# Three changes to the expert stage of an attention, FFN and expert kernel on one Trainium2 core: who makes a weight chunk's low part, who multiplies the first shares, and when weight sums are issued

## The chip, the cores and the metric

The program runs on one core of a Trainium2 chip. TensorE (PE) multiplies matrices, VectorE (DVE), ScalarE (ACT) and GpSimd (POOL) work element by element, and SyncE (SP) and POOL issue DMA transfers. The metric is the device time of one execution in microseconds. Several runs of a kernel are made and the median is taken.

## The reference

Three layers follow each other, each feeding the next. A clustered attention gives `x` of 1536 x 512. A feed-forward layer follows (512 to 2048 to 512). The third is a mixture of eight experts, and the change is in it:

```python
def _moe2_ref(x, w_gate, w1, w2) -> np.ndarray:
    N, D = x.shape
    E = w_gate.shape[1]
    logits = x @ w_gate
    logits = logits - logits.max()
    P = np.exp(logits)
    for _ in range(8):
        P /= P.sum(1, keepdims=True) + 1e-09
        P /= P.sum(0, keepdims=True) + 1e-09
        P *= N / E
    out = np.zeros((N, D), dtype=np.float32)
    for e in range(E):
        h = np.maximum(x @ w1[e], 0.0)
        ye = h @ w2[e]
        out += P[:, e:e + 1] * ye
    return out.astype(np.float32)
```

Here N = 1536, D = 512, E = 8, and w1 is 8 x 512 x 1024, w2 is 8 x 1024 x 512. The eight rounds of normalising P are called the sinkhorn steps below; a "share" is an element of P, the weight of a token for an expert.

## The kernel before

The expert stage takes the span from about 567 us to its end. It computes in fp32 out of fp32r products: each operand is split in a high part (a cast, on ACT) and a low part (the difference, an element-wise subtraction), and a product is three matmuls, high x high, high x low and low x high. Names begin with `wh`/`wl` for the first weight, `vh`/`vl` for the second, `gh`/`gl` for the activations.

The stage has 16 blocks k: two halves of the tokens (sb = k // 8), eight experts each (e = k % 8). A block has four units u. In each unit the two-by-two block product x @ w1 is made out of seven products of sums of blocks (a Strassen-like scheme); they are the seven `l1_group` calls (line 1038, six matmuls of 128x384 each), and their results leave the banks by ACT copies `c00`, `c22`, `c03`, `c44` (line 1047) and DVE sums `XA` (line 1059); `c00` and `c03` share one buffer. ACT applies the relu (lines 1057, 1061). The first weight comes in three chunks per unit, A, B, C, with two, two and three blocks of 128x256. `w1_load` (SP) fetches them, in part from sums of weights (T1 to T4) kept in DRAM, and `w1_split` makes the high part on ACT (line 967) and the low part (line 968): on DVE for A and B, on POOL for C. In even units chunk C is one tile `wf` and one operation of 128x768, in odd units two tiles (`w1r`), operations of 128x256 and 128x512.

The second layer uses seven products again. `w2_load` (SP) and `w2_add` (an accumulating DMA issued by POOL, line 992) bring the weight blocks, `w2_split` makes `vh` on ACT (line 997) and `vl` on POOL (line 998, 128x512), `g_sum` forms sums `XS`/`XA` of the activations on DVE (lines 72 and 74, 128x768), `g_split` makes `gh` on ACT (line 1018) and `gl` on DVE (line 1019, 128x768). `l2_piece` (line 1075) multiplies and DVE adds the result, times the share, to the output tile `x` (lines 1091, 1093, 1097).

For block 0 the shares are not ready when its results are, so these are stored unscaled (line 1091) and multiplied later by the shares `Pt` or their negatives `Nt`: `first_share` (line 1105), 12 products of 128x256, after the last sinkhorn step (lines 878 to 892 on DVE, and line 887 on PE, for the column sums `cs`/`cp`).

The sums of weights of the experts 4 to 7 are made by `t_step` during the first blocks: SP loads a block into a tile (`ts` for the first weight, `w2r` for the second), POOL issues a DMA that adds another block (line 227), SP stores the sum to DRAM (`td`, line 223), and so on through the list `STEPS`; a "+" stands for an accumulating DMA, a "T" for a store:

```python
STEPS = (
    ("B11", "+B12", "T1", "+B22", "T2", "+B21", "T4", "B12", "+B22", "T3"),
    ("B11", "+B12", "+B22", "T2", "+B21", "T4"),
)
```

The order of the work is set by a table: `do(t, fn, ...)` enters each piece with a place t, the table is sorted, and the pieces are emitted in that order; 28 places make a block, 7 a unit, one an `l1_group`. From the emitted order a scheduler makes the order of each engine. `behind_pe` keeps a DMA behind the last PE instruction emitted before it. Each engine then works through its list in order and waits where something is missing.

Of the kernel before, what the change touches and what calls it, by code (L numbers as in the profile page):

```python
# [7 lines left out]
F32 = mybir.dt.float32  # L8
# [3 lines left out]
AF = mybir.ActivationFunctionType  # L12
ALU = mybir.AluOpType
# [7 lines left out]
def attention_moe_moe2(ctx, tc, v, qt, kt, centroids, w_in, w_out, w_gate, w1, w2, eye, out, dbg=None):  # L21
    nc = tc.nc
# [16 lines left out]
    wp = ctx.enter_context(tc.tile_pool(name="wp", bufs=1))  # L39
# [208 lines left out]
    def w1_tiles(ch, par, nm, pool="mp"):  # L248
        sh = [P, 3 if ch == "C" else 2, KC // 2 * P]
        WT[ch] = [  # L250
            slot_pool[pool].tile(sh, F32R, tag=f"w{t}{ch}{par}", name=f"w{t}{ch}{nm}", bufs=1) for t in "hl"
        ]
        return WT[ch]

    def w1_use(T):
        return {name: T[ch] + [n] for ch in T for n, name in enumerate(MEMBERS[ch])}
# [450 lines left out]
    for i in range(NHALF):  # L707
        g = i // 4
        for t in range(HT):
            n = 6 * i + 2 * t - LEAD  # L710
# [6 lines left out]
        for s in range(NT):  # L717
            n = 6 * i + s
# [117 lines left out]
    Pt = mp.tile([P, B * NT, E], F32, tag="Pt", name="Pt", bufs=1)  # L836
    Nt = mp.tile([P, B * NT, E], F32, tag="Nt", name="Nt", bufs=1)
# [123 lines left out]
    def w1_split(k, u, ch):  # L961
        h, l = T = w1_tiles(ch, 0, f"m{k}_{u}")
        n = 0
        for src in WR[u % 2, ch]:
            m = src.shape[1]
            hs = h[:, n : n + m, :]
            nc.scalar.copy(hs, src)
            (nc.gpsimd if ch == "C" else nc.vector).tensor_tensor(l[:, n : n + m, :], src, hs.bitcast(F32), ALU.subtract)
            n += m
        W1U.setdefault((k, u), {}).update(w1_use({ch: T}))  # L970

# [129 lines left out]
    def first_share(r, c):  # L1101
        yv = xt[0].rearrange("p k s -> p (k s)").rearrange("p (m d) -> p m d", d=DM)
        for m in range(r * HT, (r + 1) * HT):
            acc = yv[:, m, c * 256 : (c + 1) * 256]
            nc.vector.tensor_scalar(acc, acc, (Nt if c else Pt)[:, m, 0:1], None, ALU.mult)

    XBLK = x_blocks(xt[1])
    XD = tc.dram_tile([len(COMBOS), P, 2, FH], F32, name="xd")
# [41 lines left out]
    def do(t, fn, *args):  # L1150
        ev2.append((t, len(ev2), fn, args))
# [4 lines left out]
    for k in range(NB):  # L1156
        for u in range(4):
            t0 = t1[k] + 7 * u
            if k or u:
                for ch, d in (("A", -12), ("B", -11), ("C", -10)):  # L1160
                    do(t0 + d, w1_load, k, u, ch)
                for ch, d in (("A", -4.6), ("B", -2.6), ("C", 0.05)):
                    do(t0 + d, w1_split, k, u, ch)
            for i in range(7):
                do(t0 + i, l1_group, k, u, i)
                if k == E - 1 and u == 3:
                    do(t0 + i + 0.9, xc_ready, PROD[i][0])
        if k == E - 1:
            for name, d in (("S1", 14), ("S2", 17), ("S4", 20.4)):
                do(t1[k] + d, xc_load, name)  # L1170
        S0 = t1[k] + G1
        sp = G1 / 14
        for p in range(2):
            r = t1[k] + 16 if p == 0 else S0 + 0.3
            for n, name in enumerate(("S1", "S2", "S3")):
                do(r + (1.0 if p == 0 else 0.25) * n, g_sum, k, name, p)
            do(S0 + 7 + 2 * p, g_sum, k, "S4", p)
        first = split_at.setdefault(k, [])
        for j in range(14):
            t = S0 + sp * (j - 3) + 0.2 if j >= 4 else S0 + 2 * j - 5.8  # L1180
            first.append(max(t, t1[k] + 9))
        for i in range(7):
            b, i_ = divmod(7 * k + i - 3, 7)
            t = split_at[b][2 * i_ + 1] + 0.15 if b >= 0 else -1
            do(t, w2_load, k, i)
            if PROD[i][1] in ("T1", "T3"):
                do(min(t + 4.4, first[2 * i] - 3.6), behind_pe, w2_add, k, i)
        for j in range(14):
            i, p = divmod(j, 2)
            do(first[j], w2_split, k, i, p)  # L1190
            do(first[j] + 0.1, g_split, k, i, p)
            for n in range(3):
                do(S0 + sp * j + sp * n / 3 + 0.01, l2_piece, k, i, p, n)
    for c, jobs in enumerate(JM):
        for j, job in enumerate(jobs):
            for n in range(len(STEPS[job[0]])):
                do(2 + 14 * c + 46 * j + 4.4 * n, behind_pe, t_step, ("gp", "wp")[c], *job, n)
    for t, fn, name in (
        (143, xc_sum, "S1"), (145, xc_sum, "S3"), (147, xc_sum, "S2"), (151, xc_sum, "S4"),
        (191, xc_halves, "A11"), (196, xc_halves, "A12"), (201, xc_halves, "A22"), (206, xc_halves, "S3"),  # L1200
# [2 lines left out]
    for n, q in enumerate(((0, 0), (0, 1), (1, 1), (1, 0))):  # L1203
        do(56.6 + 2.4 * n, first_share, *q)
# [15 lines left out]
    for n, u in enumerate(m1):  # L1220
# [3 lines left out]
        if final:  # L1224
            sums = x_sums("2_0", xt[0])
            for ch in "ABC":
                w1_load(0, 0, ch)
            plan([lambda ch=ch: w1_split(0, 0, ch) for ch in "ABC"], [(n, 1), (n, 3), (n, 4)])
        else:
            next_weights(n)  # L1230
# [26 lines left out]
    gp = slot_pool["gp"] = ctx.enter_context(tc.tile_pool(name="gp", bufs=2, reuse_waits="tile"))  # L1257
# [38 lines left out]
```

## Time and profile before

| | us |
|---|---|
| median of 3 runs | 1543.97 |
| the 3 runs | 1542.02, 1543.97, 1546.55 |
| the profiled execution | 1539.14 |
| span of the profiled execution | 1537.4 |
| mean granted TensorE clock | 0.991 |

The profile page gives the busy time of each engine and the costliest groups of instructions. Its windows give the same for any stretch of time, with the granted clock of TensorE as a share of full speed. Its timeline gives single instructions, with the idle time of the engine ahead of each and what ended that. An average over the span can hide that a short stretch has a limit of its own, so the stretches count.

### The profile page before, as it was taken

Reading aid. Unit: us, or ns where it says so; the run is one execution under the profiler, and the core shown is the slowest. Engines: PE = TensorE matmul, PEld = TensorE weight load, DVE = VectorE, ACT = ScalarE, POOL = GpSimd, SP = SyncE. Lnnn points to the kernel's source line nnn. Section 1 sums busy time; section 2 is a strip of 40 time slices with the busy share of each in tenths; the row PEclk is TensorE's granted clock in tenths of the full one; section 3 lists DMA queues with packets and bytes.
Section 4 is the critical chain, followed back from the end, with each engine's and each line's share of the span. In section 5 each row is a group of like instructions: output and inputs, shape, how many; then the busy total and the mean of one; then the engine's idle time right before and its main releaser. Section 6 shows DMA issues by size and latency. Waiting matters only on the chain.

```text
span 1537.4 us, 27389 instructions
## 1 busy us (share of the span) xinstructions
PE 1490.3 (97%) x9937; PEld 1434.6 (93%) x9937; DVE 1249.3 (81%) x1791; ACT 1029.6 (67%) x1978; POOL 827.4 (54%) x605
## 2 busy tenths in 40 slices
PE   7999989999999999999999999999999999999998
PEld 7888888889999968999999999999999999999998
DVE  5878999887564649998989998998897888888876
ACT  5878878777666646566666566766666666666663
POOL 3555555532233225467666675666666565555655
PEclk8999999999999999999999999999999999999999
DMA  8656641698867539789898997785745545636623
GB/s 218 186 129 168 166 116 54 149 252 208 225 174 190 123 76 251 199 209 241 212 211 238 240 237 207 191 232 154 193 133 145 150 130 145 160 119 159 155 62 104
DMA packets 276160, 265.48 MB, mean 173 GB/s; under 512 B 13476, under 2 KB 241528, under 8 KB 276024
## 3 DMA queue, kind: packets, MB, share of 16 engines
q1 hardware_dynamic: 237608, 217.52, 47.3%
q0 software_dynamic: 38272, 46.14, 18.8%
q8 instruction: 78, 1.28, 0.3%
q14 instruction: 58, 0.48, 0.1%
q10 hardware_dynamic: 144, 0.07, 0.0%
HBM read 207.99 MB, written 31.11 MB: 156 GB/s over the span
## 4 chain that ended last, share of the span: by engine, by line
PE 76%; DVE 12%; ACT 4%; issue 4%; DMA 2%; POOL 2%; DVEq 0%; ACTq 0%; SPq 0%; POOLq 0%
PE l0m L1038 14%; PE Ya0m L1075 10%; PE l3m L1038 7%; PE y L814 7%; PE Yb0m L1075 7%; PE p L779 7%; PE Ya1m L1075 5%; PE l1m L1038 4%; PE Yb1m L1075 4%; PE t L641 3%; PE s L589 3%; PE av L656 2%; DVE gl L1019 2%; DMA w2r<-in_moe_w_dram 1%; DVE el L648 1%
## 5 line engine op out<-in xcount | busy, mean ns | idle before, releaser
L998 POOL TENSOR_TENSOR vl<-w2r,vh 128x512 fp32r<-128x512 f32 x224 | 393.6, 1763 | 326.1 <-ACT vh L997 317.5
L1019 DVE TENSOR_TENSOR gl<-XA,gh 128x768 fp32r<-128x768 f32 x160 | 177.6, 1112 | 49.1 <-ACT gh L1018 49.0
L1018 ACT CAST gh<-XA 128x768 fp32r<-128x768 f32 x160 | 133.9, 837 | 42.0 <-PE Ya1m L1075 33.7
L997 ACT CAST vh<-w2r 128x512 fp32r<-128x512 f32 x224 | 137.6, 615 | 18.8 <-DMA w2r<-in_moe_w_dram 11.9
L1075 PE MATMUL Ya0m<-vh,gh 128*128 128x256 f32 x512 | 145.6, 284 | 1.5 <-ACT vh L997 1.5
L1075 PE MATMUL Ya0m<-vl,gh 128*128 128x256 f32 x512 | 145.6, 284 | 1.0 <-POOL vl L998 1.0
L1075 PE MATMUL Ya0m<-vh,gl 128*128 128x256 f32 x512 | 145.5, 284 | 0.0
L648 DVE TENSOR_TENSOR el<-t,eh 128x384 fp32r<-128x384 f32 x192 | 101.7, 550 | 23.1 <-ACT eh L644 20.8
L1061 ACT ACTIVATE XA<-XA 128x768 f32<-128x768 f32 x96 | 81.2, 847 | 51.7 <-DVE XA L1059 51.5
L1075 PE MATMUL Yb0m<-vh,gl 128*128 128x256 f32 x384 | 108.1, 282 | 0.0
L1075 PE MATMUL Yb0m<-vh,gh 128*128 128x256 f32 x384 | 108.1, 282 | 0.0
L1075 PE MATMUL Yb0m<-vl,gh 128*128 128x256 f32 x384 | 108.1, 281 | 0.0
L641 PE MATMUL t<-idf,E 128*128 128x128 f32 x576 | 97.7, 278 | 8.5 <-DVE el L648 5.4
L644 ACT CAST eh<-t 128x384 fp32r<-128x384 f32 x192 | 89.3, 483 | 24.3 <-PE t L641 21.0
L602 ACT ACTIVATE E<-s,sc 128x768 f32<-128x768 f32 x96 | 87.5, 912 | 19.6 <-DVE sc L597 19.0
L1075 PEld LDWEIGHTS Ya0m<-vh,gh 128*128 128x128 f32 x512 | 98.3, 192 | 1.7 <-ACT vh L997 1.7
L1075 PEld LDWEIGHTS Ya0m<-vl,gh 128*128 128x128 f32 x512 | 98.3, 192 | 1.2 <-POOL vl L998 1.2
L597 DVE TENSOR_REDUCE sc<-s 128x1 f32<-128x768 f32 x96 | 90.8, 949 | 10.2 <-PE s L589 10.2
L1075 PEld LDWEIGHTS Ya0m<-vh,gl 128*128 128x128 f32 x512 | 98.6, 193 | 0.0
L641 PEld LDWEIGHTS t<-idf,E 128*128 128x128 f32 x576 | 73.2, 143 | 22.0 <-DVE el L648 9.4
L72 DVE TENSOR_TENSOR XS<-XA,XA 128x768 f32<-128x768 f32 x32 | 60.5, 1890 | 31.7 <-ACT XA L1057 31.7
L227 POOL DMA_DIRECT2D ts<-in_moe_w_dram x44 | 55.5, 1365 | 53.7 <-DMA td<-ts 13.1
(276 smaller groups left out, 5419.7 us busy)
## 6 DMA issues: line engine op xcount, KB each, us to landing
w2r<-in_moe_w_dram SPq DMA_DIRECT2D x84, 512.0 KB, 4.8
ts<-in_moe_w_dram POOLq DMA_DIRECT2D x44, 512.0 KB, 8.0
w2r<-in_moe_w_dram POOLq DMA_DIRECT2D x44, 512.0 KB, 8.5
td<-ts SPq DMA_DIRECT2D x40, 512.0 KB, 7.1
wf<-td SPq DMA_DIRECT2D x64, 256.0 KB, 4.1
w2r<-td SPq DMA_DIRECT2D x32, 512.0 KB, 4.0
w1r<-td SPq DMA_DIRECT2D x64, 256.0 KB, 3.6
AT<-HL SPq DMA_DIRECT2D x64, 192.0 KB, 4.4
```

The costliest lines, as they stand in the source:

```text
L597: nc.vector.tensor_reduce(SC[i][:, 0, j, t : t + 1], Et[i, t][:, :, 0:CB], AX.XY, ALU.max, negate=True)
L641: nc.tensor.transpose(pt[:, t * P : (t + 1) * P], Et[i, t][:, s * P : (s + 1) * P], idf)
L644: nc.scalar.copy(eh, TT[i, s])
L648: nc.vector.tensor_tensor(el, TT.pop((i, s)), EHL[i, s].bitcast(F32), ALU.subtract)
L779: nc.tensor.matmul(ps, wt[:, s_, ks], xx[:, k_, :], start=n == 0, stop=n == 6 * nk - 1)
L814: nc.tensor.matmul(o_, wt[:, q, ms], gt[:, cols], start=first and i == 0 and st, stop=last and i == 2, skip_group_check=True,)
L997: nc.scalar.copy(h, src)
L998: nc.gpsimd.tensor_tensor(l, src, h.bitcast(F32), ALU.subtract)
L1018: nc.scalar.copy(h, src)
L1019: nc.vector.tensor_tensor(l, src, h.bitcast(F32), ALU.subtract)
L1038: nc.tensor.matmul(ps, wt[:, s_, ks], xx[:, k_, :], start=i in (0, 1, 3) and n == 0, stop=n == 3 * nk - 1, skip_group_check=True,)
L1075: nc.tensor.matmul(ps, g[:, v, ts], w[:, v, :], start=i in (0, 1, 3) and p == 0 and v == 0 and n == 0 and t != 1, stop=p == 1 and v == 1 a ...
```

## The change

Chunk C's low part is made by DVE instead of POOL, like that of A and B. The twelve products of `first_share` are an activation with scale on ACT instead of a tensor_scalar on DVE. The steps of a weight sum have places from a table, `OFFS`, instead of one each 4.4 places: a store is followed by a longer distance to the accumulating load after it. The last step of a first-weight sum moves from 39.6 to 40.5, that of a second-weight sum from 22 to 25.6.

```diff
@@ w1_split
             nc.scalar.copy(hs, src)
-            (nc.gpsimd if ch == "C" else nc.vector).tensor_tensor(l[:, n : n + m, :], src, hs.bitcast(F32), ALU.subtract)
+            nc.vector.tensor_tensor(l[:, n : n + m, :], src, hs.bitcast(F32), ALU.subtract)
             n += m
@@ first_share
             acc = yv[:, m, c * 256 : (c + 1) * 256]
-            nc.vector.tensor_scalar(acc, acc, (Nt if c else Pt)[:, m, 0:1], None, ALU.mult)
+            nc.scalar.activation(acc, acc, AF.Identity, scale=(Nt if c else Pt)[:, m, 0:1])
@@ the table
+    OFFS = (
+        (0, 4, 8, 13, 17, 22.5, 26.5, 32, 36, 40.5),
+        (0, 4.4, 8.8, 13.2, 21.2, 25.6),
+    )
     for c, jobs in enumerate(JM):
         for j, job in enumerate(jobs):
             for n in range(len(STEPS[job[0]])):
-                do(2 + 14 * c + 46 * j + 4.4 * n, behind_pe, t_step, ("gp", "wp")[c], *job, n)
+                do(2 + 14 * c + 46 * j + OFFS[job[0]][n], behind_pe, t_step, ("gp", "wp")[c], *job, n)
```

PE's order is the same in both kernels. DVE has 96 more instructions of line 968 and 12 fewer of line 1105, POOL 96 fewer, ACT 12 more, and the scheduler places their neighbours anew. Three places show it.

First, DVE at the start of block 1, in the sinkhorn steps (`rs`, `cs`, `Pt`); before:

```order
L888 TENSOR_SCALAR cs_7154<-cp_7236 128x8
L74 SCALAR_TENSOR_TENSOR XS_1_7243<-XS_1_7230,XA_1_7010 128x768
L1059 TENSOR_TENSOR XA_0_7260<-l1m_0_7253,c00m_0_7212 128x384
L1019 TENSOR_TENSOR gl_11_7233<-XA_1_7076,gh_11_7232 128x768
...
L74 SCALAR_TENSOR_TENSOR XA_1_7076<-XS_1_7243,XA_1_7076 128x768
L881 TENSOR_TENSOR Pt<-Pt,rs_7292 128x96
L1059 TENSOR_TENSOR XA_0_7336<-c44m_0_7334,c03m_0_7318 128x384
L883 TENSOR_REDUCE cs_7297<-Pt 128x8
L1019 TENSOR_TENSOR gl_21_7353<-XS_1_7243,gh_21_7352 128x768
L1059 TENSOR_TENSOR XA_0_7375<-l3m_0_7311,c22m_0_7275 128x384
```

and with the change:

```order
L888 TENSOR_SCALAR cs_7153<-cp_7236 128x8
L968 TENSOR_TENSOR wlCm_0_7223<-wf,whCm_0_7222 128x768
L1059 TENSOR_TENSOR XA_0_7260<-l1m_0_7253,c00m_0_7212 128x384
L1019 TENSOR_TENSOR gl_11_7233<-XA_1_7076,gh_11_7232 128x768
...
L1059 TENSOR_TENSOR XA_0_7336<-c44m_0_7334,c03m_0_7318 128x384
L881 TENSOR_TENSOR Pt<-Pt,rs_7292 128x96
L968 TENSOR_TENSOR wlBm_1_7358<-w1r_6773,whBm_1_7357 128x512
L883 TENSOR_REDUCE cs_7297<-Pt 128x8
L1059 TENSOR_TENSOR XA_0_7374<-l3m_0_7311,c22m_0_7275 128x384
L74 SCALAR_TENSOR_TENSOR XA_1_7076<-XS_1_7243,XA_1_7076 128x768
```

Chunk C's low part takes the place of the first sum of line 74, which moves behind gl; of the later ones, gl_21 moves ahead of the sinkhorn step and the sum behind both XA.

Second, DVE behind the last sinkhorn step, where the first shares stood; before:

```order
L892 TENSOR_SCALAR Nt<-Pt 128x96
L1105 TENSOR_SCALAR x_69<-x_69,Pt 128x256 x2
L1019 TENSOR_TENSOR gl_10_7966<-XA_0_7375,gh_10_7965 128x768
L1059 TENSOR_TENSOR XA_1_7768<-l3m_3_7887,c22m_3_7873 128x384
L1105 TENSOR_SCALAR x_69<-x_69,Pt 128x256
L1091 COPY x_69<-Ya0m_0_7214 128x256 x2
L1105 TENSOR_SCALAR x_69<-x_69,Nt 128x256 x4
L1091 COPY x_69<-Ya1m_0_7215 128x256
L72 TENSOR_TENSOR XS_1_8016<-XA_1_7726,XA_1_7783 128x768
```

and with the change:

```order
L892 TENSOR_SCALAR Nt<-Pt 128x96
L1019 TENSOR_TENSOR gl_10_7966<-XA_0_7374,gh_10_7965 128x768
L1059 TENSOR_TENSOR XA_1_7768<-l3m_3_7887,c22m_3_7873 128x384
L74 SCALAR_TENSOR_TENSOR XA_0_7374<-XS_0_7709,XA_0_7374 128x768
L1091 COPY x_69<-Ya0m_0_7214 128x256 x2
L1091 COPY x_69<-Ya1m_0_7215 128x256
L968 TENSOR_TENSOR wlCm_0_8010<-wf,whCm_0_8009 128x768
L72 TENSOR_TENSOR XS_1_8017<-XA_1_7726,XA_1_7783 128x768
```

The products by `Pt` and `Nt` are gone from between the copies of line 1091, a sum of line 74 stands ahead of them now, and wlC ahead of the sum of line 72.

Third, POOL in block 3, at the second weight's low parts and two DMAs of weight sums; before:

```order
L998 TENSOR_TENSOR vl_41_9811<-w2r_6770,vh_41_9810 128x512
L227 DMA w2r_6771<-in_moe_w_dram 128x4x256
L968 TENSOR_TENSOR wlCm_2_9856<-wf,whCm_2_9855 128x768
L998 TENSOR_TENSOR vl_50_9860<-w2r_6771,vh_50_9859 128x512
L998 TENSOR_TENSOR vl_51_9909<-w2r_6771,vh_51_9908 128x512
L227 DMA ts_6_9015<-in_moe_w_dram 128x2x512
L998 TENSOR_TENSOR vl_60_9967<-w2r_6770,vh_60_9966 128x512
```

and with the change:

```order
L998 TENSOR_TENSOR vl_41_9811<-w2r_6770,vh_41_9810 128x512
L998 TENSOR_TENSOR vl_50_9859<-w2r_6771,vh_50_9858 128x512
L998 TENSOR_TENSOR vl_51_9908<-w2r_6771,vh_51_9907 128x512
L227 DMA w2r_6771<-in_moe_w_dram 128x4x256
L998 TENSOR_TENSOR vl_60_9966<-w2r_6770,vh_60_9965 128x512
L227 DMA ts_6_9015<-in_moe_w_dram 128x2x512
L998 TENSOR_TENSOR vl_61_10015<-w2r_6770,vh_61_10014 128x512
```

The two accumulating DMAs (line 227) stand one or two low parts later, and wlC is gone.

## Rows read from the trace of the kernel before

**Rows 1.** Page, part 1: busy time, share of the span and instructions of each engine

```profile
PE 1490.3 (97%) x9937; PEld 1434.6 (93%) x9937; DVE 1249.3 (81%) x1791; ACT 1029.6 (67%) x1978; POOL 827.4 (54%) x605
```

**Rows 2.** Windows: us, busy us (instructions) of PE, PEld, DVE, ACT, POOL, granted clock, DMA share, GB/s

```profile
540.00:1537.40 997.40, 978.50 (x6841) 963.02 (x6839) 845.60 (x1112) 638.99 (x1105) 598.47 (x380) 0.99 0.67 175
600.00:620.00 20.00, 16.30 (x115) 15.89 (x115) 19.79 (x32) 8.61 (x17) 11.26 (x9) 1.00 1.17 264
666.00:672.00 6.00, 6.00 (x34) 6.00 (x34) 6.00 (x10) 2.47 (x5) 2.48 (x1) 0.72 1.02 257
```

**Rows 3.** Timeline of PE: start, us, operation, [idle before <- what ended it]

```profile
584.32 0.44 PE L1038 MATMUL l0m<-chS,wlCm 128*128 128x384 f32 x1 [0.67 <-POOL wlCm L968]
...
610.86 0.39 PE L887 MATMUL cp<-cs,ones_f 128*128 128x8 f32 x2 [1.38 <-DVE cs L883]
...
616.12 0.44 PE L1038 MATMUL l1m<-chA,whAm 128*128 128x384 f32 x1 [2.31 <-DVE XA L1059]
...
665.48 0.38 PE L1075 MATMUL Ya1m<-vh,gh 128*128 128x256 f32 x1 [1.86 <-DVE x L1091]
...
807.84 0.45 PE L1038 MATMUL l3m<-chS,whCm 128*128 128x384 f32 x1 [0.65 <-ACT c03m L1047]
...
824.42 0.45 PE L1038 MATMUL l3m<-chS,whCm 128*128 128x384 f32 x1 [1.20 <-ACT c03m L1047]
...
878.62 0.44 PE L1038 MATMUL l0m<-chS,whBm 128*128 128x384 f32 x1 [0.79 <-ACT c00m L1047]
...
893.23 0.44 PE L1038 MATMUL l1m<-chA,whAm 128*128 128x384 f32 x1 [1.71 <-DVE XA L1059]
...
1515.81 0.38 PE L1075 MATMUL Ya0m<-vh,gh 128*128 128x256 f32 x1 [1.52 <-ACT vh L997]
```

**Rows 4.** Timeline of DVE, single instructions of the expert stage

```profile
594.82 0.95 DVE L1019 TENSOR_TENSOR gl<-XA,gh 128x768 fp32r<-128x768 f32 x1
...
597.67 3.82 DVE L74 SCALAR_TENSOR_TENSOR XS<-XS,XA 128x768 f32<-128x768 f32 x1
...
610.72 4.88 DVE L1019 TENSOR_TENSOR gl<-XS,gh 128x768 fp32r<-128x768 f32 x1
...
661.35 3.74 DVE L1105 TENSOR_SCALAR x<-x,Nt 128x256 f32<-128x256 f32 x4
...
815.32 6.35 DVE L74 SCALAR_TENSOR_TENSOR XS<-XS,XA 128x768 f32<-128x768 f32 x1
...
1172.09 2.32 DVE L72 TENSOR_TENSOR XS<-XA,XA 128x768 f32<-128x768 f32 x1 [2.45 <-ACT XA L1057]
```

**Rows 5.** Timeline of POOL, single instructions of the expert stage

```profile
581.98 2.29 POOL L968 TENSOR_TENSOR wlCm<-wf,whCm 128x768 fp32r<-128x768 f32 x1
...
597.61 3.04 POOL L968 TENSOR_TENSOR wlCm<-wf,whCm 128x768 fp32r<-128x768 f32 x1
...
661.50 1.91 POOL L968 TENSOR_TENSOR wlCm<-wf,whCm 128x768 fp32r<-128x768 f32 x1 [0.90 <-ACT whCm L967]
...
890.05 3.00 POOL L968 TENSOR_TENSOR wlCm<-w1r,whCm 128x256 fp32r<-128x256 f32 x2
```

**Rows 6.** Lines 968 and 967: min/median/max ns; who made engines wait, us, times

```profile
L968 POOL TENSOR_TENSOR wlCm<-w1r,whCm x64: 722/1288/2023, 571.8 to 1483.2; 128x256 fp32r<-128x256 f32 x32, 128x512 fp32r<-128x512 f32 x32
...
L968 POOL TENSOR_TENSOR wlCm<-wf,whCm x32: 1826/1852/3045, 480.5 to 1466.7; 128x768 fp32r<-128x768 f32 x32
...
L968 DVE TENSOR_TENSOR wlBm<-wf,whBm x32: 677/1243/1558, 531.9 to 1460.3; 128x512 fp32r<-128x512 f32 x32
...
L968 DVE TENSOR_TENSOR wlBm<-w1r,whBm x32: 677/684/1298, 568.3 to 1476.1; 128x512 fp32r<-128x512 f32 x32
...
  ACT whCm L967: 33.3, 30
...
  ACT whBm L967: 14.4, 26
...
L967 ACT CAST whCm<-w1r x64: 390/508/624, 571.3 to 1481.1; 128x256 fp32r<-128x256 f32 x32, 128x512 fp32r<-128x512 f32 x32
```

## The prediction, made before the changed kernel ran

> **What bounds the kernel now.** I read the page first: PE is busy 97% of the span, DVE 81%, ACT 67% [rows 1]. So the question is not how long an engine works but where PE stands still. The windows come next: in the expert stage and what follows (540 us to the end) PE works 978.5 of 997.4 us and DVE 845.6, which is 85% [rows 2]. Between 600 and 620 us the picture is another: DVE 19.79 of 20 us, PE 16.30. And from 666 to 672 us PE is busy all the time, but the granted clock is 0.72. The timeline of PE then names the single gaps with what ended each [rows 3]; they are the whole budget of a change that takes no matmul away. The ones that bear on it: 0.67 us at 584 (POOL's low part of chunk C late), 1.38 and 2.31 at 611 and 616 (DVE late, in the sinkhorn steps and in an XA sum), 1.86 at 665 (DVE late in emptying a result bank), 0.65 at 808, 1.20 at 824, 0.79 at 879, 1.71 at 893 and 1.52 at 1516.
>
> Why DVE is late is in its timeline [rows 4]. The 128x768 difference gl takes 0.95 us when it runs alone, as at 594.82. At 597.67 a sum of the same size takes 3.82, at 610.72 the same difference 4.88, at 661.35 four small products take 3.74, at 815.32 a sum takes 6.35. POOL's timeline has the partner of the first and third of these four [rows 5]: wlC from 597.61 for 3.04 us, wlC from 661.50 for 1.91. And at 890.05 two wlC pieces take 3.00 us just before the gap at 893. When both engines work on operands in SBUF, one stands while the other finishes, and a long POOL instruction makes a short DVE one long.
>
> The Trainium skill says why: in "SBUF — State Buffer", section "Who interferes with whom", DVE and GpSimd share one pair of ports, and it is held as an exclusive lock, so that the loser waits entirely. This trace agrees: 0.95 us alone, 4.88 beside POOL.
>
> **Part 1, chunk C's low part moves from POOL to DVE.** Removed from POOL: 32 pieces of 128x768 at a median of 1.85 us and 64 smaller ones at 1.29 [rows 6], about 142 us. Added to DVE: the same 96. DVE's own price: 0.95 us for 128x768 with two inputs in SBUF [rows 4], 0.68 for 128x512 (wlB from w1r) [rows 6]; 256 columns more cost 0.27, so I take 0.41 for 128x256, an estimate from these two. That is 32 x 0.95 + 32 x (0.68 + 0.41) = 65 us. Beside POOL's remaining vl it can be more: wlB in the even units has a median of 1.24 against 0.68, 0.56 on top, which would make it 32 x 0.56 = 18 us dearer, 83 us as the upper end. DVE's share in the stage goes from 85% to (845.6 + 65)/997.4 = 91%, at the upper end 93%, less what it no longer loses to wlC. So there is cover, but less of it, and in a busy block no more than a us or two.
>
> What it gives back, gap by gap. (a) 584: POOL starts wlC at 581.98 and needs 2.29 us for it [rows 5]; DVE at 0.95 would be done before PE's need at 583.65 if it starts at the same time, but it has other work. So 0 to 0.67, I take 0.6. (b) 611 and 616, together 3.69: in the new order of DVE the sums XS, wlC and gl stand in other places (the first order of the change section), and 597.67 and 610.72, 3.82 + 4.88 against 2 x 0.95, hold 6.8 us of blocking, the first under wlC. DVE gets wlC itself in that stretch, 0.95 + 1.09. If half of the 6.8 goes, 3.4, less 2.0 of wlC, DVE is 1.4 us earlier at least; if all goes it is 4.8 earlier and both gaps close. I take 2.9, bounds 1.4 and 3.69. (c) 824: the row names ACT's copy c03; it has one buffer with c00 and waits until DVE's XA sum has read that. The sum L74 ahead of it took 6.35 from 815, 5.4 us over its own length, under wlC and two vl queued behind it. Without wlC one of the three is left out, and XA comes about 2 us earlier: 1.2, bounds 0.4 and 1.2. (d) 893: 1.71 us, XA late behind a wlC pair of 3.00 us at 890.05; DVE has the pair itself now, 1.09. I take 1.0, bounds 0 and 1.71. (e) 808 waits for a copy that stands behind a slow DMA landing, 879 for a sum under vl, 1516 for vh of the last block: none has wlC in it, 0.
>
> **Part 2, the first expert's shares move from DVE to ACT.** Twelve products of 128x256 leave DVE. They go to ACT, where a 128x256 copy takes 0.39 us, the smallest of the copies of chunk C [rows 6]: 12 x 0.39 = 4.7 us over some 17 us of a stage in which ACT works 639 of 997 us [rows 2]. That is hidden by ACT's idle time; were it not, 0.4 us would fall on the next gh. On DVE the four at 661.35 stood directly ahead of the copy that frees the bank for which PE waited 1.86 us, and PE's clock then fell from full speed to its lower level: 6 us at 0.72 lose 6 x 0.28 = 1.7 us [rows 2]. Both go, 3.56 us; bounds 1.86 (the clock dips anyway) and 3.56. In DVE's new order the copies follow gl, XA and one sum (second order), 2.4 us of work where 661.35 alone took 3.74.
>
> **Part 3, the transposed-weight sums keep distance behind the stores.** No DMA is added or removed; POOL issues the accumulating load later, so that it no longer stands at the head of POOL's queue for the store. In the third order two of them move behind one or two vl, which are made earlier; the store of the sum comes later. The tightest place in the tables is the last expert's: its last store moves from 179.6 to 180.5, and the load of chunk C that reads it stands at 186. A place is 2.2 us (997 us for 16 blocks of 28), so 12 us lie between. I cost the part at 0: this slack hides it. If it is gone, a load lands late, as at 808, 0.65 per case; bounds -0.8 (the gap at 879) and +1.5.
>
> **The sum.** -0.6 - 2.9 - 1.2 - 1.0 - 3.56 = -9.3. On the other side stand new stalls: DVE at 91% is late more often. Now 0.65 + 1.20 + 0.79 + 1.71 = 4.4 us of gaps fall in the 800 us after 680; DVE's idle time there shrinks from 15 to 9 in a hundred. Nothing shows that price. From 0 to about as much again, 5; I take 1.5, near the low end, because the wlC is needed late in a unit (the fifth of seven products) and POOL's locks are fewer. That leaves -7.7: the profiled execution goes from 1539.1 to 1531.4. Its time lies 4.8 us below the median of the three runs, 1543.97, so the median goes to **1536.3**.
>
> **Rivals.** *The lock only moves* (0.19). DVE makes in 65 us what it lost before, and gaps (a) to (d) stay or come back elsewhere; only the shares pay: -3.56, 1540.4. For it: DVE already waits more where it is busiest. Against: the product of two blocked engines is gone, since POOL needed 142 us. The Trainium skill speaks on this side: "Perfetto Trace Analysis", section "Optimizing Scalar/DVE Operations", says that moving work between GPSIMD and DVE might not help as they share a port. By that sentence the gain would be that of the shares alone; the trace has wlC slower on POOL than a like piece on DVE, 1.85 against 0.95.
>
> *DVE stands still for ACT's cast* (0.08), slower. DVE goes in order: wlC has to wait for whC from ACT, and what is behind it, L72's sum, XA and the copies out of the result banks, waits along. POOL waited 33.3 us in 30 pieces for it, and DVE itself 14.4 in 26 for whB, 0.55 each [rows 6]. If 0.5 us of it reach PE in each of 32 even units, that is +16 against -9.3: +6.7, 1550.7. The place is ahead of the sum at 1172.09: DVE has 2.45 us of idle time there [rows 4], so it decides when wait and piece together come to more than that. Against it: this idle time, and the piece on POOL held up that very sum, 2.32 against 0.95.
>
> *Everything closes* (0.10): 0.67 + 3.69 + 3.56 + 0.65 + 1.20 + 0.79 + 1.71 = 12.3 and no new stall: 1531.7. Against: (e).
>
> *Given back* (0.13): the change does what it says, but DVE's new stalls reach the upper end of 5 us, and one or two weight blocks land late, 3 us: -9.3 + 8 = -1.3, 1542.7.
>
> **How the numbers follow.** The forecast has 0.50, from 1533.5 to 1539.2. A change under 0.3%, 4.6 us, can't be told from none here, so faster is under 1539.3 and slower over 1548.6. Faster: 0.48 of the forecast, 0.10, 0.05 of the first rival (0.63). Slower: 0.07 of the second, 0.01 of the last (0.08). The rest is the same, 0.29. The range from 1531 to 1543.5 takes in all but the second rival, half of the last, and the outer ends.
>
> **What would show it.** Right: in the new timeline of PE no gap over 0.5 us at 584, 665 and 893, at most 1 us in sum at 605 to 620, the clock from 666 to 672 at 1; in DVE's wlC of 128x768 a median of 0.95 to 1.3; no gl or L74 over 3.5 us. Wrong: a run of new gaps of 0.3 to 0.6 us in PE, one per even unit, ended by DVE; or DVE's total over 930 us after 540; or a gap at 600 to 620 as long as before.

## The result, and the profile after

The changed kernel takes 1521.53 us (median of four runs, 1519.73 to 1527.11), the kernel before beside it 1544.97. The ratio is 0.9863, with a 95% interval of 0.9839 to 0.9887: 23.4 us faster. The forecast was 7.7 us. The direction was right, the size a third of what came, and the time lies below the range. Two later comparisons of the same two kernels gave 15.2 and 17.9 us (in the experiments below), so 23.4 is the largest of three.

The profiled execution of the changed kernel took 1522.13 us, against 1539.14 before, so the two profiles differ by 17.0 us. The page's first part of the changed kernel stands beside [rows 1]; POOL lost 171 us of work and DVE gained only 14:

```profile
PE 1485.0 (98%) x9937; PEld 1430.6 (94%) x9937; DVE 1263.4 (83%) x1875; ACT 1032.9 (68%) x1990; POOL 656.0 (43%) x509
```

The windows of the changed kernel (columns as in [rows 2]; the first one ends at 1480 us, ahead of the tail):

```profile
540.00:1480.00 940.00, 938.74 (x6574) 925.90 (x6573) 830.90 (x1155) 626.49 (x1092) 403.58 (x271) 1.00 0.69 182
600.00:620.00 20.00, 20.00 (x145) 20.00 (x144) 18.49 (x37) 11.47 (x22) 10.19 (x8) 1.00 1.15 280
666.00:672.00 6.00, 6.00 (x45) 6.00 (x44) 6.00 (x8) 4.71 (x10) 4.84 (x4) 1.00 1.03 193
```

PE is busy in all of 600 to 620 us, where [rows 2] had 16.30 of 20, and the granted clock from 666 to 672 is 1.00, where it was 0.72. The timeline of PE has five gaps over 0.15 us left in the whole expert stage, against thirteen before (nine of them are in [rows 3]). Three of the five stand in the tail, at 1484, 1501 and 1503, one of 0.17 us at 850, and the last of them is

```profile
738.13 0.44 PE L1038 MATMUL l0m<-chS,whCm 128*128 128x384 f32 x1 [1.00 <-ACT c22m L1047]
```

The gaps at 584, 611, 616, 665, 808, 824, 879 and 893 of [rows 3] have no counterpart. That at 738 is new. The first and the last matmul of layer 1 in the expert stage (line 1038; the first stands some 10 us ahead of the 567 us given above for the stage), before:

```profile
556.62 0.34 PE L1038 MATMUL l0m<-chA,whAm 128*128 128x384 f32 x1
...
1495.02 0.34 PE L1038 MATMUL l0m<-chA,wlCm 128*128 128x384 f32 x1
```

and after:

```profile
556.37 0.34 PE L1038 MATMUL l0m<-chA,whAm 128*128 128x384 f32 x1
...
1481.11 0.34 PE L1038 MATMUL l0m<-chA,wlCm 128*128 128x384 f32 x1
```

From 938.40 us it went to 924.74: 13.7 us of the 17.0 lie between these two matmuls. 0.25 us lie ahead of the stage. The rest, 3.1 us, lies behind the last of them, where the change does nothing (no chunk C, no share, no weight sum); 2.6 us of it are a low clock in the profile before (0.55 from 1517 to 1524 us), which the profile of the control below does not have.

**Where DVE's time came from.** The groups of DVE by shape, from 540 to 1480 us (columns: busy us, mean ns, idle before them); before:

```profile
L74 DVE SCALAR_TENSOR_TENSOR XS<-XS,XA 128x768 f32<-128x768 f32 x31 | 61.9, 1997 | 1.0
...
L72 DVE TENSOR_TENSOR XS<-XA,XA 128x768 f32<-128x768 f32 x31 | 59.5, 1920 | 31.7 <-ACT XA L1057 31.7
...
L1059 DVE TENSOR_TENSOR XA<-c44m,c03m 128x384 f32<-128x384 f32 x63 | 48.9, 776 | 7.2 <-ACT c44m L1047 5.6
...
L968 DVE TENSOR_TENSOR wlAm<-w1r,whAm 128x512 fp32r<-128x512 f32 x32 | 32.0, 1001 | 0.0
...
L1019 DVE TENSOR_TENSOR gl<-XA,gh 128x768 fp32r<-128x768 f32 x149 | 160.6, 1079 | 42.8 <-ACT gh L1018 42.8
...
L72 DVE TENSOR_TENSOR XA<-XA,XA 128x768 f32<-128x768 f32 x31 | 33.9, 1092 | 0.0
```

after, with the new group's three shapes:

```profile
L74 DVE SCALAR_TENSOR_TENSOR XS<-XS,XA 128x768 f32<-128x768 f32 x31 | 32.7, 1056 | 0.0
...
L72 DVE TENSOR_TENSOR XS<-XA,XA 128x768 f32<-128x768 f32 x31 | 40.3, 1301 | 0.6 <-ACT XA L1057 0.6
...
L1059 DVE TENSOR_TENSOR XA<-c44m,c03m 128x384 f32<-128x384 f32 x64 | 37.0, 578 | 10.7 <-ACT c44m L1047 9.1
...
L968 DVE TENSOR_TENSOR wlAm<-w1r,whAm 128x512 fp32r<-128x512 f32 x32 | 24.9, 777 | 0.0
...
L1019 DVE TENSOR_TENSOR gl<-XA,gh 128x768 fp32r<-128x768 f32 x153 | 176.7, 1155 | 36.1 <-ACT gh L1018 36.1
...
L72 DVE TENSOR_TENSOR XA<-XA,XA 128x768 f32<-128x768 f32 x31 | 43.3, 1398 | 0.0
...
L968 DVE TENSOR_TENSOR wlCm<-wf,whCm 128x768 fp32r<-128x768 f32 x31 | 30.4, 981 | 24.9 <-ACT whCm L967 24.9
...
L968 DVE TENSOR_TENSOR wlCm<-w1r,whCm 128x512 fp32r<-128x512 f32 x32 | 25.0, 780 | 0.3 <-ACT whCm L967 0.2
...
L968 DVE TENSOR_TENSOR wlCm<-w1r,whCm 128x256 fp32r<-128x256 f32 x32 | 22.6, 705 | 2.0 <-ACT whCm L967 2.0
```

DVE has 78.0 us of new work (30.4 + 25.0 + 22.6). But the sum L74 XS fell from 61.9 to 32.7 us and the sum L72 XS from 59.5 to 40.3: 48.4 us, and 19 more from the two rows below them. The last two rows of the first list rose, gl from 160.6 to 176.7 (with four more in the window) and XA from 33.9 to 43.3. In the same window of the kernel before DVE was busy

```profile
540.00:1480.00 940.00, 928.72 (x6475) 914.05 (x6474) 806.52 (x1061) 613.79 (x1066) 566.15 (x361) 1.00 0.69 180
```

806.5 us, after 830.9: 24.4 us more, not 65. And the changed kernel gets further in the window: between the first and the last matmul of layer 1, where the work is the same, DVE is busy 808.8 us before and 824.9 after, 16.1 more.

One even unit shows how the two sums came free. Before, POOL's 128x768 piece (from 1171.75 us for 1.85) ran beside the sum of line 72, which took the 2.32 us of [rows 4], and the vl queued behind the piece ran beside the sum of line 74; in POOL's and DVE's timelines:

```profile
1173.54 2.02 POOL L998 TENSOR_TENSOR vl<-w2r,vh 128x512 fp32r<-128x512 f32 x1
...
1174.45 1.93 DVE L74 SCALAR_TENSOR_TENSOR XS<-XS,XA 128x768 f32<-128x768 f32 x1
```

After, the piece is gone from POOL, a gl stands ahead of the sum of line 74 in DVE's order and meets that vl, and the sum takes 0.94:

```profile
1158.69 2.04 POOL L998 TENSOR_TENSOR vl<-w2r,vh 128x512 fp32r<-128x512 f32 x1 [1.80 <-ACT vh L997]
...
1159.49 2.05 DVE L1019 TENSOR_TENSOR gl<-XA,gh 128x768 fp32r<-128x768 f32 x1
```

By the starts and ends in these timelines, the piece overlapped the sum of line 72 in 25 of 31 units, but that of line 74 in only 2, the two cases of [rows 4]; a vl overlapped the sum of line 74 in 29 of 31 units before and in 10 after. So part of the time that the sums gave back went to other operations, as the rise of gl shows.

### The profile page after: what moved, and what is told of

It reads as the page before. It is cut to its first block, busy times and chain, and to the rows that moved or that the text cites. A ratio compares the mean times of both kernels' runs of the same rounds, so it can differ in the third digit from the quotient of the medians.

```text
span 1520.4 us, 27347 instructions
## 1 busy us (share of the span) xinstructions
PE 1485.0 (98%) x9937; PEld 1430.6 (94%) x9937; DVE 1263.4 (83%) x1875; ACT 1032.9 (68%) x1990; POOL 656.0 (43%) x509
## 4 chain that ended last, share of the span: by engine, by line
PE 83%; DVE 6%; ACT 4%; issue 3%; DMA 3%; POOL 1%; SPq 0%; DVEq 0%; ACTq 0%; POOLq 0%
PE l0m L1038 17%; PE Ya0m L1075 11%; PE l3m L1038 8%; PE Yb0m L1075 8%; PE y L814 7%; PE p L779 7%; PE Ya1m L1075 6%; PE l1m L1038 4%; PE Yb1m L1075 4%; PE t L641 3%; PE s L589 2%; PE av L656 2%; ACT E L602 1%; DVE el L648 1%; DMA w2r<-in_moe_w_dram 1%
## 5 line engine op out<-in xcount | busy, mean ns | idle before, releaser
L998 POOL TENSOR_TENSOR vl<-w2r,vh 128x512 fp32r<-128x512 f32 x224 | 355.8, 1595 | 502.6 <-ACT vh L997 499.1
L1019 DVE TENSOR_TENSOR gl<-XA,gh 128x768 fp32r<-128x768 f32 x160 | 188.9, 1182 | 39.7 <-ACT gh L1018 39.6
L602 ACT ACTIVATE E<-s,sc 128x768 f32<-128x768 f32 x96 | 87.5, 911 | 19.7 <-DVE sc L597 19.3
L656 PE MATMUL av<-eh,VV 128*128 128x384 f32 x192 | 80.0, 417 | 0.3
```

What stands on the lines that cost most here:

```text
L602: nc.scalar.activation(e.rearrange("p (a c) -> p a c", a=2), Et[i, t][:, :, 0:CB], AF.Exp, bias=sc[:, 0, j, t : t + 1], scale=1.0, accum_o ...
L656: nc.tensor.matmul(AVt[i], st.VV[j][:, s, :], m, start=s == 0 and n == 0, stop=s == NT - 1 and n == 1)
L998: nc.gpsimd.tensor_tensor(l, src, h.bitcast(F32), ALU.subtract)
L1019: nc.vector.tensor_tensor(l, src, h.bitcast(F32), ALU.subtract)
```

## The experiments

Each kernel's time is compared with runs of the kernel before on the same chip. Sixteen runs were made, in four groups; some repeat a kernel. The edits are shown shortened: `l[...]` stands for `l[:, n : n + m, :]`, and `.bitcast(F32)` is left out. Every version gets its own order from the scheduler, so no run changes an engine and keeps all the rest in place.

### The parts alone

The control is the kernel before, unchanged.

> The kernel before once more, as a control, to see what a profile of it on the same chip shows. Theory A (closed gaps and clock): the timed runs of before lie 4.8 us above its profiled execution because in other executions PE's clock falls at more of the same gaps; then this profile has a mean clock at or below 0.991 and PE gaps in the expert stage of 13 to 17 us, and the times are 1542 to 1547. Theory B (the profiled execution was just another chip's): this profile is near the timed median, with the same gaps and the same clock.

Measured: 1539.77 us beside 1541.03 for the other runs of it, ratio 0.9996 [0.9964, 1.0028]. The single runs spread from 1532.7 to 1549.5. This profile has 18.2 us of PE gaps in the stage, where the first had 14.3, and layer 1 takes 942.6 us from first to last matmul, where it took 938.4. Most of the difference lies at one place. In DVE's, POOL's and PE's timeline there:

```profile
611.75 1.28 POOL L227 DMA_DIRECT2D w2r<-in_moe_w_dram  x1 [3.05 <-DMA td<-w2r]
...
611.91 4.73 DVE L1059 TENSOR_TENSOR XA<-c44m,c03m 128x384 f32<-128x384 f32 x1
...
612.52 1.80 POOL L998 TENSOR_TENSOR vl<-w2r,vh 128x512 fp32r<-128x512 f32 x1
...
613.75 2.46 POOL L968 TENSOR_TENSOR wlCm<-w1r,whCm 128x256 fp32r<-128x256 f32 x2
...
616.92 0.60 PE L887 MATMUL cp<-cs,ones_f 128*128 128x8 f32 x2 [6.54 <-DVE cs L883]
```

In the first profile this XA began at 610.02, and POOL issued the same DMA behind it:

```profile
610.25 1.28 POOL L227 DMA_DIRECT2D w2r<-in_moe_w_dram  x1 [3.46 <-DMA td<-w2r]
```

XA took 0.55 us there, and the difference behind it the 4.88 us [rows 4]. Here XA begins 0.16 us behind the DMA's issue, 0.6 us ahead of vl, and takes 4.73 for 0.55, until vl and both pieces of wlC are done. The sinkhorn sum waits behind that, and PE stands 6.54 us at once, not 1.38 and 2.31. Then the clock falls:

```profile
616.00:624.00 8.00, 7.08 (x30) 7.08 (x31) 6.95 (x18) 2.28 (x4) 0.76 (x2) 0.56 0.89 203
```

8 us at 0.56, mostly the lower of the clock's two levels, lose 3.5 us. None of theory A's numbers came (times of 1542 to 1547, gaps of 13 to 17 us, a mean clock of 0.991 or less), but its idea holds: gaps and clock vary between executions, here with 0.4 us of order between two engines. The mean clock over the span, 0.992, says nothing of it. XA would have been done before vl began; that POOL's issue of the DMA is part of the hold is what this looks like, but no run tests it.

Part 1 alone (on the kernel before):

```diff
-(nc.gpsimd if ch == "C" else nc.vector).tensor_tensor(l[...], src, hs, ALU.subtract)
+nc.vector.tensor_tensor(l[...], src, hs, ALU.subtract)
```

> Only chunk C's low part moves from POOL to DVE; shares stay on DVE, weight sums keep their places. Theory A (POOL's long instruction held DVE up at nearly every gap): 9 to 14 us faster than before, 1530 to 1536; the gaps at 611, 616, 824 and 893 are gone, that at 665 stays or shrinks, as no wlC lies under the shares. Rival (the lock only moves, DVE's load eats it): within 3 us of before, gaps of the same sum in other places.

Measured: 1521.76 us, ratio 0.9886 [0.9824, 0.9948], 19.3 us faster. This is more than expected, and as far as the whole change goes, though four runs give a wide interval, 8 to 27 us. Layer 1 takes 926.3 us, 12 to 16 less than in the two profiles of the kernel before. Of the old gaps only the one under the shares has a successor; PE's timeline:

```profile
671.01 0.45 PE L1038 MATMUL l1m<-chA,whAm 128*128 128x384 f32 x1 [1.40 <-DVE XA L1059]
...
678.80 0.44 PE L1038 MATMUL l0m<-chS,whCm 128*128 128x384 f32 x1 [0.84 <-ACT c22m L1047]
```

The rival, that the lock only moves, has fallen.

Part 2 alone:

```diff
-nc.vector.tensor_scalar(acc, acc, (Nt if c else Pt)[:, m, 0:1], None, ALU.mult)
+nc.scalar.activation(acc, acc, AF.Identity, scale=(Nt if c else Pt)[:, m, 0:1])
```

> Only the first expert's shares move from DVE to ACT. Theory A: 3 to 4 us faster than before, the gap of 1.86 us at 665 and the clock's fall behind it are gone, all other gaps stay. Rival (the gap is due to wlC's hold and another DVE piece takes the place of the shares): under 1 us faster.

Measured: 1534.68 us, ratio 0.9958 [0.9933, 0.9983], 6.4 us faster. The gap at 665 and the fall of the clock behind it are gone, those at 610 and 616 stand at 1.41 and 2.42 us as in [rows 3]. But behind this pair of gaps the clock falls here, which it did not in the first profile:

```profile
616.00:620.00 4.00, 4.00 (x20) 4.00 (x19) 3.79 (x12) 0.62 (x1) 1.36 (x2) 0.59 1.18 246
```

The 6.4 us may in part be such variation; the interval is 2.6 to 10.3.

Part 3 alone:

```diff
-do(2 + 14 * c + 46 * j + 4.4 * n, behind_pe, t_step, ...)
+do(2 + 14 * c + 46 * j + OFFS[job[0]][n], behind_pe, t_step, ...)
```

> Only the places of the weight sums change. Prediction as on record: no change, bounds -0.8 and +1.5 us. Rival (the sums are what held POOL's queue, so that wlC and two vl came in one piece at 816): the gaps at 808, 824, 831 and 879 shrink, 2 to 4 us faster.

Measured: 1539.67 us, ratio 0.9994 [0.9963, 1.0025]. No change, as expected. Its profile has 5.03 us of gap at 616, where the control had 6.54, and a new one of 4.10 at 748.

### The change without one part

> The changed kernel once more, as the base of this group on its chip: 1519 to 1524, gaps of PE in the expert stage of 3 to 5 us in sum.

Measured: 1526.30 us (1522.57 to 1528.34) beside 1541.49 for the kernel before, ratio 0.9898 [0.9877, 0.9918]; 2.6 us of PE gaps in the stage; 924.7 us from the first to the last matmul of layer 1, as in the first profile. The gain is 15.2 us here, not 23.4.

Without part 3:

```diff
-do(2 + 14 * c + 46 * j + OFFS[job[0]][n], behind_pe, t_step, ...)
+do(2 + 14 * c + 46 * j + 4.4 * n, behind_pe, t_step, ...)
```

> The change without its third part (weight sums at their old places). Theory A: within 2 us of the whole change, since the sums pay nothing. Rival (the sums pay where DVE is loaded more): 3 us or more behind it, with a gap near 600 to 620 or 730 to 750.

Measured: 1522.77 us, ratio 0.9870 [0.9850, 0.9890]. Not behind the whole change, but 3.5 us ahead of it, which neither theory had.

Without part 2:

```diff
-nc.scalar.activation(acc, acc, AF.Identity, scale=(Nt if c else Pt)[:, m, 0:1])
+nc.vector.tensor_scalar(acc, acc, (Nt if c else Pt)[:, m, 0:1], None, ALU.mult)
```

> The change without its second part (shares stay on DVE). With part 1 alone the shares left gaps of 1.40 and 0.84 us at 671 and 679, which the whole change does not have. Theory A: 1.5 to 3.5 us behind the whole change. Rival (DVE has room for them): within 1 us.

Measured: 1526.23 us, ratio 0.9903 [0.9884, 0.9922], level with the whole change by the times. In the profile layer 1 takes 928.1 us against 924.7, with gaps of 1.49, 0.84 and 1.40 us at 675, 682 and 707 that the whole change doesn't have. The 3.4 us are of the expected size; that the times don't show them stays open.

Without part 1:

```diff
-nc.vector.tensor_tensor(l[...], src, hs, ALU.subtract)
+(nc.gpsimd if ch == "C" else nc.vector).tensor_tensor(l[...], src, hs, ALU.subtract)
```

> The change without its first part (chunk C's low part stays on POOL). Theory A: it keeps the gaps at 611 to 617, 824 and 893 and lies at 1532 to 1537, 12 to 16 us behind the whole change. Rival (shares and sums together are worth more than each alone): under 9 us behind it.

Measured: 1541.30 us, ratio 1.0007 [0.9986, 1.0028]: 15.0 us behind the whole change, as theory A said, but nothing is left of the gain, not even that of the shares. Its profile has the old gaps at 812, 834, 882 and 896, and new ones; two of PE's:

```profile
742.10 0.69 PE L1038 MATMUL l1m<-chA,whAm 128*128 128x384 f32 x1 [3.65 <-DVE XA L1059]
...
1047.15 0.45 PE L1038 MATMUL l1m<-chA,whAm 128*128 128x384 f32 x1 [2.35 <-DVE XA L1059]
```

At 611, where the kernel before stood longest, it has 0.26 us. So with POOL's long pieces in place, moving others about brings gaps up elsewhere; this fits the run of part 3 alone.

### DVE's load by itself, and the halves of part 1

The low part made twice by DVE:

```diff
-nc.vector.tensor_tensor(l[...], src, hs, ALU.subtract)
+for _ in range(2 if ch == "C" else 1):
+    nc.vector.tensor_tensor(l[...], src, hs, ALU.subtract)
```

> The change, but DVE makes chunk C's low part twice, the second time over the first: a price for DVE's load alone, some 65 us more of it, which brings DVE from 88% to about 94% of the expert stage. The record's rival and its 1.5 us for new stalls rest on DVE's load. If load decides: 10 us or more slower than the whole change, with new gaps all over the stage. If POOL's hold decides and load does not: under 4 us slower.

Measured: 1546.59 us, ratio to the kernel before 1.0037 [1.0019, 1.0054]; against the changed kernel of the same group, 1522.69, it is 23.9 us slower. Load decides. The window from 540 to 1480 us of this kernel:

```profile
540.00:1480.00 940.00, 926.00 (x6417) 909.73 (x6416) 862.11 (x1223) 607.48 (x1065) 396.15 (x267) 0.99 0.69 180
```

DVE is busy 862 us, 31 us more than after the change, and PE loses 13 us of work in the same window. Nineteen gaps stand in PE's timeline of the stage, 16.6 us in sum, the longest 3.29 us at 869, and several of 0.35 between 829 and 1077, where the change has one of 0.17. Those in layer 1 end with DVE's sums, a column sum or ACT's copies, none with wlC itself, so it is not wlC's own lateness that PE meets. DVE, busy 92% of the window, can no longer hide the added work.

The odd units' pieces back on POOL, then (the mirror) the even units' piece:

```diff
-nc.vector.tensor_tensor(l[...], src, hs, ALU.subtract)
+(nc.gpsimd if ch == "C" and u % 2 else nc.vector).tensor_tensor(l[...], src, hs, ALU.subtract)
```

```diff
-nc.vector.tensor_tensor(l[...], src, hs, ALU.subtract)
+(nc.gpsimd if ch == "C" and u % 2 == 0 else nc.vector).tensor_tensor(l[...], src, hs, ALU.subtract)
```

> The change, but the odd units' two pieces of chunk C (128x256 and 128x512) go back to POOL; the even units' 128x768 stays on DVE. Theory A (each wlC of POOL that comes in one piece with a vl holds DVE up): the gaps that followed the odd units' pieces, at 611 to 617 in part and at 893, come back, 2 to 6 us slower than the whole change. Rival (only the long 128x768 does harm): within 1.5 us.

Measured: 1523.73 us, ratio 0.9884 [0.9858, 0.9910], 1.0 us behind the whole change on its chip (1522.69). That is the rival's number, and no gap came back at 611 to 617 or 893. The whole change gains 17.9 us over the kernel before here, this kernel 16.8.

> The mirror of the run before: the even units' 128x768 of chunk C goes back to POOL, the odd units' two pieces stay on DVE. If the 128x768 piece does the harm, since it falls together with the two sums of lines 72 and 74 that each even unit has: 1534 to 1540, nearly all of the gain lost, and a mean of L74 XS near 2.0 us as before (1.06 with the whole change). If both halves do equal harm: 1528 to 1532.

Measured: 1531.36 us beside 1539.03 for the kernel before, ratio 0.9952 [0.9935, 0.9969]: 7.7 us faster, half of the 15.3 that parts 1 and 2 bring on the same chip (1523.71). It lies below 1534 to 1540 and in the range that I gave for equal harm, 1528 to 1532. But with the even piece alone 16.8 of 17.9 us came, so the halves do no equal harm, and their gains do not add up. The sums tell the halves apart. DVE's groups with the odd pieces alone on DVE:

```profile
L74 DVE SCALAR_TENSOR_TENSOR XS<-XS,XA 128x768 f32<-128x768 f32 x31 | 58.3, 1880 | 1.0
...
L72 DVE TENSOR_TENSOR XS<-XA,XA 128x768 f32<-128x768 f32 x31 | 64.5, 2081 | 31.3 <-ACT XA L1057 31.3
```

and with the even piece alone:

```profile
L74 DVE SCALAR_TENSOR_TENSOR XS<-XS,XA 128x768 f32<-128x768 f32 x31 | 33.5, 1082 | 0.0
...
L72 DVE TENSOR_TENSOR XS<-XA,XA 128x768 f32<-128x768 f32 x31 | 40.3, 1300 | 0.6 <-ACT XA L1057 0.6
```

With the even piece on POOL both sums are as long as before; with it on DVE both are short. The gaps at 827, 874 and 888 are back, too, in the first.

The kernel before with POOL's wlC cut into pieces of 128x256:

```diff
-(nc.gpsimd if ch == "C" else nc.vector).tensor_tensor(l[...], src, hs, ALU.subtract)
+for q in range(m) if ch == "C" else ():
+    nc.gpsimd.tensor_tensor(l[:, n + q], src[:, q], h[:, n + q], ALU.subtract)
+if ch != "C":
+    nc.vector.tensor_tensor(l[...], src, hs, ALU.subtract)
```

> The kernel before with each wlC of POOL cut into pieces of 128x256 (three in all units), nothing else: POOL's work is the same or a little more, but no piece is longer than some 0.7 us alone. If DVE's wait is for the one POOL instruction in progress, DVE gets in between the pieces and most of the gaps close: 1525 to 1535. If POOL, once on, keeps DVE out over several of its instructions in a row: no gain, 1538 to 1546.

Measured: 1551.44 us, ratio 1.0073 [1.0054, 1.0091], 12.4 us slower than before. Neither theory said so. DVE's timeline ahead of one of its gaps (this kernel's lines are numbered up to 3 higher):

```profile
866.19 1.49 DVE L1022 TENSOR_TENSOR gl<-XS,gh 128x768 fp32r<-128x768 f32 x1
867.61 1.07 DVE L1062 TENSOR_TENSOR XA<-c44m,c03m 128x384 f32<-128x384 f32 x1
```

and POOL's:

```profile
865.69 3.57 POOL L969 TENSOR_TENSOR wlCm<-w1r,whCm 128x256 fp32r<-128x256 f32 x3
```

Here DVE gets in between the pieces: two of its instructions run under three of POOL's, each 0.5 us longer than alone (0.95, 0.55). Elsewhere in the same profile it does not, and one difference is held over two vl and the three pieces between them:

```profile
612.08 5.88 DVE L1022 TENSOR_TENSOR gl<-XS,gh 128x768 fp32r<-128x768 f32 x1
...
613.25 2.65 POOL L969 TENSOR_TENSOR wlCm<-w1r,whCm 128x256 fp32r<-128x256 f32 x3
```

So neither theory holds everywhere: DVE waits for one POOL instruction in some places and for a row of them in others. The groups, from 540 to 1480 us, show what the cut did:

```profile
L74 DVE SCALAR_TENSOR_TENSOR XS<-XS,XA 128x768 f32<-128x768 f32 x30 | 41.6, 1386 | 0.9
...
L72 DVE TENSOR_TENSOR XS<-XA,XA 128x768 f32<-128x768 f32 x30 | 38.9, 1296 | 27.7 <-ACT XA L1060 27.7
...
L72 DVE TENSOR_TENSOR XA<-XA,XA 128x768 f32<-128x768 f32 x30 | 51.7, 1722 | 0.0
```

The two sums XS got short, as the first theory wants (1997 and 1920 ns before). But the sums XA of line 72 went from 1092 to 1722 ns, those of line 74 from 1461 to 1819, and the short XA sums of 128x384 with `c44`, `c03` stayed about as they were (776 before, 717 here). POOL's pieces came to 182 us in the window, after 138, and the order changed on both engines. So the hold moved to other operations; which of these makes the 12 us stays open.

### A version against both

Parts 1 and 2 without part 3 were run again beside the whole change:

> The changed kernel, as the base of this group: 1519 to 1527, and once more a short gap of PE near 739, which the runs so far had at 1.00 and 0.63 us.

> Parts 1 and 2 with the weight sums at their old places. Theory A' (the new places of the sums cost a stall near 740, where the load of a sum and two vl fall together): no gap near 739, 1 to 4 us faster than the whole change. Rival (they are equal, and the first comparison was chance): within 1 us.

Measured: 1522.69 us (0.9872 [0.9845, 0.9900]) for the whole change, 1519.48 us (0.9862 [0.9838, 0.9885]) without part 3. Both comparisons put it ahead, by 3.5 and 3.2 us, but the intervals overlap, and the profiles do not carry so much: layer 1 takes 924.7 or 924.8 us in all three profiles of the change, 923.1, 924.2 and 924.5 in three without part 3. The gap at 738 to 741 (1.00, 0.64, 1.03 us) is in each profile with part 3 and in none without; in two of the three without, one of 1.13 and 0.97 us stands at 616 and 621 instead. So part 3 swaps one gap of 1 us for another.

The even piece alone on DVE, with part 2 and without part 3:

```diff
-nc.vector.tensor_tensor(l[...], src, hs, ALU.subtract)
+(nc.gpsimd if ch == "C" and u % 2 else nc.vector).tensor_tensor(l[...], src, hs, ALU.subtract)
```

> A candidate to beat both: the even units' wlC on DVE, the odd units' on POOL, shares on ACT, weight sums at their old places. DVE has 27 us less to do in the stage than with the whole of part 1. If DVE's load still costs: 1 to 3 us faster than parts 1 and 2 alone, below. If the odd pieces' hold costs the same as their work: within 1 us.

> Parts 1 and 2 alone, as the base of this group on its chip: 1518 to 1524.

Measured: 1526.24 us (0.9912 [0.9898, 0.9927]) against 1523.71 us (0.9890 [0.9874, 0.9906]) for parts 1 and 2 whole. 2.5 us slower, not faster, though the intervals overlap; its profile has a gap of 3.32 us at 621. By the medians the best is parts 1 and 2 without part 3, ahead of the kernel before by 15 to 21 us in three groups.

## Why the prediction was wrong

**The base of the sum.** All gaps were read off one profiled execution. It was 5.8 us below the median that stood beside the result, and I took that as an offset that both kernels would have (4.8 by the three runs I had). No run supports that. Three profiled executions of the changed kernel lie 0.6 us above, 3.7 below and 4.7 above the medians of their groups, while layer 1 takes the same time in each; what varies there lies ahead of layer 1, which starts at 556.4, 558.1 and 559.6 us, and in the tail. In the kernel before, layer 1 varies too: the control's gap at 617 was 6.54 us with 3.5 us of low clock behind it, where the first profile had 3.69 and no fall. Against the two profiles of before, layer 1 got 13.7 and 17.9 us shorter, which is near the 15.2 and 17.9 us of the two later comparisons. The 6.4 us by which the first comparison exceeds its two profiles (23.4 - 17.0) did not come again. The kernel before had its highest median there, 1544.97, where the other groups have 1539.0 to 1541.5; why is open.

**Part 1, terms (a) to (d).** That these gaps close was right, each term too small. From the start of each matmul in both profiles: (a) 0.8 us for 0.6; (b) 4.0 for 2.9; (c) 1.5 for 1.2; (d) 1.9 for 1.0. In sum 8.2 against 5.7.

**Term (e), put at nothing.** I put 808 and 879 at 0, as no wlC was in them, and left 831 out, a gap of 0.2. They gave 0.7, 0.9 and 0.5 us, and none of them is in the profile of part 1 alone either. That is 2.1 us for 0. That a gap's last wait does not name wlC did not mean that it was free of it: without wlC, POOL's and DVE's other work comes at other times.

**Part 2.** 3.56 forecast, 3.7 us found at 665 to 670 in the two profiles, 1.7 of it the clock. By itself it gave 6.4, together with part 3 and without part 1 nothing: the shares pay only if no other gap comes up in their place.

**Part 3.** 0 forecast; no effect alone, a gap of 1 us at 738 against one at 616 in the whole. There DVE's pieces ran beside two vl; DVE's, POOL's and ACT's timelines of the change:

```profile
729.81 4.51 DVE L968 TENSOR_TENSOR wlCm<-w1r,whCm 128x256 fp32r<-128x256 f32 x2 [1.22 <-ACT whCm L967]
...
730.71 3.05 POOL L998 TENSOR_TENSOR vl<-w2r,vh 128x512 fp32r<-128x512 f32 x2
...
736.86 0.84 ACT L1061 ACTIVATE XA<-XA 128x768 f32<-128x768 f32 x1 [4.42 <-DVE XA L1059]
```

XA came late, ACT's relu and the copy c22 behind it, and PE stood 1.00 us.

**What DVE gets back, the step that failed.** By the gaps inside layer 1 the forecast was 7.7 us, and 13.7 came. The term for new stalls is not where it failed: 1.5 us taken, 1.0 found at 738 and about 0.3 each near 654 and 860. It failed in what the gaps give back, (e) put at nothing and (b) and (d) taken at only a part. Behind both stands one step: the prediction said that DVE would be 91% busy, "less what it no longer loses to wlC", left that unpriced, and for (b)'s lower bound even took wlC's 2.0 us off the gain. It is most of the price: the pieces added 78.0 us and the shares took 7.3 away, yet DVE's busy time in the window rose by 24.4, so 46 us came back (55 over the same work). From 540 us to the end DVE is 88% busy (861.4 of 980.4), not 91. The two sums of the even units, 1997 and 1920 ns on the mean for 0.95 us alone, stood in the groups by shape of the kernel before. I went by four single cases and not by these groups, and the two cases of line 74 among them were the only two in which wlC itself lay beside that sum.

That a higher load of DVE has a price was right: the doubled part costs 24 us.

**The rivals.** That the lock only moves was worth 0.19; part 1 alone gave 19.3 us and refutes it as a whole, though part of the hold did move, from the sums to gl. The sentence cited for it, of the Trainium skill's "Perfetto Trace Analysis", section "Optimizing Scalar/DVE Operations", says only that such a move might not help; here it did: POOL's piece was twice as long as DVE's (1.85 against 0.96 us), and it ran beside one of DVE's sums, the vl behind it beside the other. That DVE waits for ACT's cast was right as a fact: 24.9 us of idle time ahead of the 128x768 piece in the rows above. It cost nothing, because the 31.7 us of idle time that stood ahead of L72 before went to 0.6. One even unit of the change:

```profile
1157.75 0.96 DVE L968 TENSOR_TENSOR wlCm<-wf,whCm 128x768 fp32r<-128x768 f32 x1 [2.03 <-ACT whCm L967]
...
1158.62 0.95 DVE L72 TENSOR_TENSOR XS<-XA,XA 128x768 f32<-128x768 f32 x1
```

The wait ends with the cast, the piece takes 0.96 us, and the sum behind it its 0.95, where [rows 4] had 2.32. The rival that everything closes came nearest in its gaps, 12.3 us against 13.7, and had a chance of 0.10.

**The 3.1 us behind the last layer-1 matmul** are no part of the change. The tail took 42.3 us in the first profile of the kernel before, 40.0 in the control, and 39.3, 38.0 and 41.2 in three of the change: it varies by itself.

## What to carry to other kernels

Before an elementwise operation is moved between two engines that hold each other up, compare each group's mean with the duration of the same shape alone: the surplus over all groups, not the gaps that a view names, bounds what the move can free. Not all of it comes free, since the other engine's remaining work then meets other operations. Half of the work moved here, one piece per even unit, gave 16.8 of 17.9 us in one group and 12.8 of 15.3 in another, so try the parts of a move by themselves. And take two profiles of the kernel before, and compare the stretch that the change touches: a gap that depends on which of two engines comes first by less than 1 us is not a constant, and neither is what lies ahead of the stretch and behind it.

## What the runs showed of the hardware that was not expected

Shorter POOL instructions did not simply let DVE in. Cut into 128x256, they did so at 866 us, but at 612 us one difference of DVE took 5.88 us beside two vl and the three pieces between them; the kernel became 12.4 us slower, for reasons that stay open. Five of the six DVE instructions over 2.6 us between 560 and 1500 us in the profile of the kernel before, and the two of 4.73 and 5.88 us above, have a DMA issued by POOL within them or just ahead; no run tests whether that is the cause.

And a stall of PE was followed by a low clock in some executions and not in others at the same place in the program: behind 3.69 us in two pieces at 611 to 616 the granted clock stayed at 1.00 (600 to 620 us in [rows 2]), behind 3.83 us in the same two pieces, with part 2 alone, it was 0.59 for 4 us, and behind 6.54 us in one piece, in the control, 0.56 for 8 us.
